# One pool of eight PSUM banks, and the scores of two query tiles in one stretch, in an attention kernel with a mixture of experts

## The chip, the cores and the metric

The kernel runs on one core of a Trainium2 chip. Its engines work side by side, each through its own queue in order: TensorE (PE; its weight loads are shown apart as PEld), VectorE (DVE), ScalarE (ACT), GpSimd (POOL) and SyncE (SP), which issues the DMAs. TensorE writes to PSUM alone, which has eight banks of 512 float32 columns by 128 partitions; VectorE and ScalarE read from there. The metric is the time of the device in microseconds. Everything here is float32.

## The reference: what is computed

Two blocks in a row, over 4 batches of 1088 rows. The first is a linear attention with a sketch of the features; its output, 128 columns wide, is the input `x` of the second: causal attention by four experts, of which each row uses the two with the largest gate.

```python
a = einsum('rd,bhsd->bhsr', S1, x); b = einsum('rd,bhsd->bhsr', S2, x)   # phi: 64 products a row
...
num = einsum('bhsf,bhfd->bhsd', q_p, kv); den = einsum('bhsf,bhf->bhs', q_p, z)[..., None] + 1e-06
x = num / den                                   # (B, S, H*D) = (4, 1088, 128)
for e in range(4):                              # experts, 64 wide
    q = x @ wq[e]; k = x @ wk[e]; v = x @ wv[e]
    scores = where(causal, -1e9, (q @ k.T) / 8)
    a = exp(scores - scores.max(-1)); a /= a.sum(-1) + 1e-09
    out += gate[e] * (a @ v @ wo[e])            # gate: softmax over the two best of x @ w_gate
```

## The kernel before: tiling, order and names

**Tiles.** The experts are taken in two pairs (`g` = 0, 1; the two of a pair are `e` = 0, 1, one in partitions 0 to 63, the other in 64 to 127). The 1088 queries of a batch are cut into tiles `i` of 128: eight whole ones and one of 64. Two whole tiles (2p, 2p+1) form a group `p`. For tile `i` the scores cover the keys 0 to 128 (i + 1), since later ones are masked.

**Steps of one tile.** `scores` (L400) makes the products of queries and keys in PSUM (`sc`, L412), in pieces of 512 keys. `soften` (L393) reads them once on VectorE (L395: adds the mask, writes the negated scores to `a` in SBUF and their minimum to `mx`) and once on ScalarE (L398: the exponential, with its sum in `z`). `turns_of` (L469) transposes `a` on TensorE, up to four blocks of 128 x 128 into one bank `tp` (L477), and `evacuate` copies the bank to `aT` in SBUF: two copies of three on ScalarE (L72), the third on VectorE (L70). `values` (L546) multiplies `aT` by the values into a bank `av` (L552), `gates` (L494) makes the factors (gate over sum, product on POOL at L501) and transposes them into the same bank (L507), ScalarE copies these to `rs` (L509), and VectorE multiplies `av` by `rs` into `yT` (L557), which frees the bank. `output` (L614) projects `yT` through `wo` into a bank `po` (L619), and the copy of it goes out by a DMA of SP.

**PSUM.** Two pools. `ps_sc` has two buffers of two banks each, for scores alone; a tile of more than 512 keys takes both, one for each expert. `ps_tp` has four buffers of one bank, for everything else: transposes, values, outputs, and all steps that prepare the next batch (`kps`, `qps`, `tq`, `num`, `tx`, `qk`, `vg` and others, in `prepare`, L206).

**Units.** TensorE's order is written out by hand; the other engines' order is made by the framework's scheduler. A batch is a list of units (`units`, L529):

- "Q": tiles 0 and 1, both expert pairs (`scores_first`, L421)
- "P": tiles 2 and 3 of one pair
- "G": a larger group (tiles 4 and 5, or 6 and 7) of one pair
- "L": the last tile of 64 rows, both pairs at once (`scores_last`, L441)

Batches 0 to 2 run Q, P, P, G, G, G, G, L. The last batch runs P, P, A, B, A, B, L, A, B, A, B, Q, where "A" and "B" are the two tiles of a large group as units of their own. For each unit the loop does: scores (for "G" of the first tile alone), values of units that are ready, for "G" the scores of its second tile, and then the `jobs`: transposes left over from the unit before, output projections, and for "G" the transposes of its first tile; between the jobs stand pieces of the preparation of the next batch (`spend`). Then "G" transposes its second tile. "A" and "B" transpose half of their tile at once and leave the other half to the next unit. "L", and "Q" of the last batch, run the jobs left over before their own scores. In the last batch the preparation's pieces are used up in the first two units.

Of the kernel before, what the change touches and what calls it, by code (L numbers as in the profile page):

```python
# [10 lines left out]
F32 = mybir.dt.float32  # L11
BF16 = mybir.dt.bfloat16
I32 = mybir.dt.int32
ALU = mybir.AluOpType
ACTF = mybir.ActivationFunctionType
# [4 lines left out]
def kernel(  # L20
# [20 lines left out]
    nc = tc.nc  # L41
    B, H, S, D = q.shape
# [7 lines left out]
    NG = E // 2  # L50
    scale = 1.0 / math.sqrt(HD)
# [3 lines left out]
    p4 = ctx.enter_context(tc.tile_pool(name="p4", bufs=4))  # L55
    ps_sc = ctx.enter_context(tc.tile_pool(name="ps_sc", bufs=2, space=bass.MemoryType.PSUM))
    ps_tp = ctx.enter_context(tc.tile_pool(name="ps_tp", bufs=4, space=bass.MemoryType.PSUM))

# [8 lines left out]
    def evacuate(out_, in_):  # L67
        turn[0] += 1
        if turn[0] % 3 == 0:
            nc.vector.tensor_copy(out_, in_)  # L70
        else:
            nc.scalar.copy(out_, in_)  # L72


# [110 lines left out]
    mask = const("mask", [128, 1024], BF16)  # L185
# [20 lines left out]
    def prepare(b):  # L206
# [6 lines left out]
        n = NJ - 1  # L213

        def bank(name):
            return ps_tp.tile([128, 512], F32, tag="tp", name=name)

# [174 lines left out]

    def soften(a, src, msk, mx, z, most=3e38):  # L393

        nc.vector.tensor_tensor_reduce(out=a, in0=src, in1=msk, scale=-1.0, scalar=most,  # L395
                                       op0=ALU.add, op1=ALU.min, accum_out=mx)
        if z is not None:
            nc.scalar.activation(out=a, in_=a, func=ACTF.Exp, bias=mx, scale=-1.0, accum_out=z)  # L398

    def scores(b, i, g, qk, z):  # L400

        n = 128 * i + 128
        if n <= 512:
            t = ps_sc.tile([128, 2, 512], F32, tag="sc", name=f"sc{b}_{i}_{g}")
            sc = [t[:, e, :] for e in range(2)]
        else:
            sc = [ps_sc.tile([128, 1024], F32, tag="sc", name=f"sc{b}_{i}_{g}_{e}") for e in range(2)]
        for c0 in range(0, n, 512):
            c1 = min(c0 + 512, n)
            for e in range(2):  # L410
                rows = slice(64 * e, 64 * e + 64)
                nc.tensor.matmul(sc[e][:, c0:c1], qk[rows, g, 128 * i : 128 * i + 128], qk[rows, NG + g, c0:c1],  # L412
                                 start=True, stop=True)
        mx = p4.tile([128, 2], F32, tag="mx", name=f"mx{b}_{i}_{g}")
        width, tag, bufs = (512, "as", 8) if n <= 512 else (S, "a", 4)
        ats = [p4.tile([128, width], F32, tag=tag, name=f"a{b}_{i}_{g}_{e}", bufs=bufs) for e in range(2)]
        for e in range(2):
            soften(ats[e][:, 0:n], sc[e][:, 0:n], mask[:, 1024 - n :], mx[:, e : e + 1], z[:, e : e + 1])
        return ats

    def scores_first(b, qk, zs):  # L421

        made = [[[], []] for _ in range(NG)]
        for g in range(NG):
            t = ps_sc.tile([128, 2, 512], F32, tag="sc", name=f"sc{b}_0_{g}")
            for i in range(2):
                for e in range(2):
                    rows = slice(64 * e, 64 * e + 64)
                    nc.tensor.matmul(t[:, e, 128 * i : 256 * i + 128], qk[rows, g, 128 * i : 128 * i + 128],  # L429
                                     qk[rows, NG + g, 0 : 128 * i + 128], start=True, stop=True)  # L430
            mx = p4.tile([128, 2, 2], F32, tag="mx0", name=f"mx{b}_0_{g}")
            a = [p4.tile([128, 512], F32, tag="as", name=f"a{b}_0_{g}_{e}", bufs=8) for e in range(2)]
            for i in range(2):
                for e in range(2):
                    n, dst = 128 * i + 128, a[e][:, 128 * i : 256 * i + 128]
                    soften(dst, t[:, e, 128 * i : 256 * i + 128], mask[:, 1024 - n :], mx[:, i, e : e + 1],
                           zs[g][:, i, e : e + 1])
                    made[g][i].append(dst)
        return made

    def scores_last(b, qk, z):  # L441

        sc = [ps_sc.tile([128, 1024], F32, tag="sc", name=f"sc{b}_8_{e}") for e in range(2)]
        ext = [ps_tp.tile([128, 512], F32, tag="tp", name=f"ext{b}_{e}")[:, 0:64] for e in range(2)]

        def some(dst, e, c0, c1):
            rows = slice(64 * e, 64 * e + 64)
            for g in range(NG):
                nc.tensor.matmul(dst[64 * g : 64 * g + 64], qk[rows, g, 1024:], qk[rows, NG + g, c0:c1],  # L449
                                 start=True, stop=True)  # L450

        for e in range(2):
            some(ext[e], e, 1024, S)
        for c in range(0, 1024, 512):
            for e in range(2):
                some(sc[e][:, c : c + 512], e, c, c + 512)
        mx = p4.tile([128, 4], F32, tag="mx8", name=f"mx{b}_8")
        ats = [p4.tile([128, S], F32, tag="a", name=f"a{b}_8_{e}") for e in range(2)]
        for e in range(2):
            soften(ats[e][:, 1024:], ext[e], mask_last, mx[:, 2 + e : 3 + e], None)  # L460
        for e in range(2):

            most = mx[:, e : e + 1]
            nc.vector.tensor_tensor_reduce(out=ats[e][:, 0:1024], in0=sc[e], in1=mask[:, 0:1].to_broadcast([128, 1024]), scale=-1.0,
                                           scalar=mx[:, 2 + e : 3 + e], op0=ALU.add, op1=ALU.min, accum_out=most)
            nc.scalar.activation(out=ats[e], in_=ats[e], func=ACTF.Exp, bias=most, scale=-1.0, accum_out=z[:, e : e + 1])
        return ats

    def turns_of(name, i, ats, aT, q0):  # L469

        def some(e0, e1, j0, j1):
            tp = ps_tp.tile([128, 512], F32, tag="tp", name=f"tp{name}_{e0}_{j0}")
            nk, nj = size(j0), j1 - j0
# [55 lines left out]
    def units(b, qk, vt, gw, gw8):  # L529
# [3 lines left out]


        for p in range((NJ - 1) // 2) if b < B - 1 else (1, 3, 2, 0):
# [3 lines left out]
            for g in range(NG):  # L539
# [6 lines left out]
                def values(p=p, g=g, aT=aT, yT=yT, name=name):  # L546
                    av = ps_tp.tile([128, 512], F32, tag="tp", name=f"av{name}")
                    for j in range(2 * p + 2):
# [22 lines left out]
                if p == 0:  # L571
                    four.append((z, turns, close))
                elif p == 1:
                    yield "P", make, turns, [close]
                elif b < B - 1:
                    yield "G", make, turns, [close]
                else:
                    yield "A", make, turns, []
                    yield "B", make, turns, [close]
            if four:  # L580
# [6 lines left out]
    def last_unit(b, qk, vt, gw8):  # L587
# [5 lines left out]
        def values():  # L593
            av = ps_tp.tile([128, 512], F32, tag="tp", name=f"av{b}_8")
            for g in range(NG):
# [18 lines left out]
    def output(b, p, yT):  # L614
        nq, n = (128, 2) if p < NJ // 2 else (64, 1)
        po = ps_tp.tile([128, 512], F32, tag="tp", name=f"po{b}_{p}")
        for x in range(n):
# [9 lines left out]
    with tc.manual_schedule(engines={mybir.EngineType.PE}):  # L627

        warm = ps_tp.tile([128, 512], F32, tag="tp", name="warm")
        for _ in range(16):  # L630
# [13 lines left out]
        for b in range(B):  # L644
# [16 lines left out]
            for n, (kind, make, turned, close) in enumerate(units(b, *now)):  # L661
                jobs, turns = turns + done, []
                if kind == "L" or kind == "Q" and b == B - 1:
                    for f in jobs:
                        f()
                    jobs = []
                    groups += turning
                    turning = []
                made = {x: make(x) for x in ((0, 1) if kind == "P" else (1,) if kind == "B" else (0,))}
                ends = do_values()  # L670
                spend(0.0, columns=True)
                if kind == "G":
                    made[1] = make(1)
                    jobs += turned(made, 0)
                done = [f for finish, to_gate in ends for f in finish(to_gate)]
                if b + 1 < B:
# [10 lines left out]
                if kind == "G":  # L687
                    turns = turned(made, 1)
                    cut = len(turns)
                else:  # L690
                    turns = [f for x in made for f in turned(made, x)]
                    cut = len(turns) // 2 if kind in "AB" and len(turns) > 2 else 0
                for f in turns[:cut]:
                    f()
                turns = turns[cut:]
                (groups if kind == "G" else turning).extend(f() for f in close)
# [39 lines left out]
```

## Time and profile before

| | |
|---|---|
| median of 3 runs | 398.3 us (398.27 to 398.81) |
| profiled execution, its time | 398.61 us |
| its span, first to last instruction | 396.8 us |
| busy from 0 to 40 us (start-up): TensorE, VectorE, ScalarE | 34.2, 30.0, 15.0 us |
| busy from 40 to 311.8 us (271.8 us) | 261.1, 160.2, 161.4 us |
| busy from 311.8 us to the end (last batch, 85.0 us) | 77.9, 44.5, 50.2 us |

How to read what follows: rows of the page's groups have the line, the engine, the operation, output and inputs by name, shapes, the count, then busy time and mean ns of one, then the idle time of the engine just before and what ended it. A float32 product shows as two rows on TensorE, and the rows of the two experts run side by side in two halves of the array. The length of a TensorE row holds its way through the array, so rows overlap and a busy TensorE need not be streaming at its best.

These are the largest groups of score work on the page's account and in the list of groups by shape:

| group | count | mean ns | busy us |
|---|---|---|---|
| transposes `tp`, 128 x 128 | 640 | 276 | 89.1 |
| values `av`, 256 columns | 512 | 384 | 62.0 |
| scores `sc`, 512 columns | 192 | 624 | 51.3 |
| copies `aT` on ScalarE, 512 columns | 85 | 586 | 47.8 |
| copies `aT` on VectorE, 512 columns | 43 | 690 | 29.7 |
| exponential, all shapes | 128 | 767 | 98.1 |

### The profile page before, as it was taken

How to read it: one execution, taken by the hardware profiler on the slowest of the kernel's cores; microseconds unless marked ns; L12 is line 12 of the kernel's file. 1: busy time of each engine (PE TensorE's matmuls, PEld its weight loads, DVE VectorE, ACT ScalarE, POOL GpSimd, SP SyncE). 2: the span in 40 equal slices, each digit the busy share in tenths (PEclk: the TensorE clock that was granted, in tenths of full speed). 3: DMA queues.
4: the chain of work that ended last, by engine and by line, in shares of the span. 5: the costliest groups of instructions: out<-in, count | busy, mean ns of one | idle time of the engine just before them, and what ended most of it. 6: DMA issues, size and time to landing. Idle time of an engine off the chain costs nothing.

```text
span 396.8 us, 8017 instructions
## 1 busy us (share of the span) xinstructions
PE 373.2 (94%) x3152; PEld 265.4 (67%) x3152; DVE 234.6 (59%) x661; ACT 226.5 (57%) x550; POOL 58.7 (15%) x87
## 2 busy tenths in 40 slices
PE   8898999999999999999999999999999999999995
PEld 7764687667665776767664767766756475666673
DVE  6867866555548675366456564555655844745551
ACT  2236666555666656456475656754665565656582
POOL 3400461000001740000000541000000010000010
PEclk9999999999999999999999999999999999999999
DMA  7705022000000000000000000000000000000000
GB/s 192 200 2 170 16 98 71 2 1 15 13 2 0 15 2 5 15 0 15 1 15 0 2 13 7 13 2 0 15 13 2 1 16 6 0 15 2 15 4 26
DMA packets 11349, 9.95 MB, mean 25 GB/s; under 512 B 3632, under 2 KB 10288, under 8 KB 11312
## 3 DMA queue, kind: packets, MB, share of 16 engines
q1 hardware_dynamic: 11296, 9.44, 8.6%
q8 instruction: 24, 0.39, 0.4%
q14 instruction: 13, 0.11, 0.1%
q10 hardware_dynamic: 16, 0.00, 0.0%
HBM read 7.22 MB, written 2.23 MB: 24 GB/s over the span
## 4 chain that ended last, share of the span: by engine, by line
PE 72%; DVE 15%; ACT 9%; issue 2%; DMA 2%; SPq 0%; ACTq 0%; DVEq 0%
PE av L552 16%; PE sc L412 15%; PE tp L477 14%; DVE a L395 7%; ACT a L398 7%; PE qk L326 5%; PE vg L338 3%; PE num L300 3%; PE po L619 3%; PE av L600 3%; PE sc L449 2%; DMA qin<-in_q_dram 2%; DVE qT L223 1%; PE sc L429 1%; PE qps L251 1%
## 5 line engine op out<-in xcount | busy, mean ns | idle before, releaser
L398 ACT ACTIVATE a<-a,mx 128x256 f32<-128x256 f32 (+7 forms) x128 | 98.1, 767 | 59.6 <-DVE mx L395 59.2
L395 DVE CUSTOM_DVE_ANT_0 a<-sc,mask 128x256 f32<-128x256 f32 (+7 forms) x128 | 90.2, 754 | 64.1 <-PE sc L412 62.1
L477 PE MATMUL tp<-ident,a 128*128 128x128 f32 (+1 forms) x648 | 90.1, 276 | 10.6 <-DVE yT L557 6.8
L477 PEld LDWEIGHTS tp<-ident,a 128*128 128x128 f32 (+1 forms) x648 | 72.8, 142 | 26.0 <-DVE yT L557 10.2
L72 ACT COPY aT<-tp 128x512 f32<-128x512 f32 (+3 forms) x119 | 61.6, 544 | 17.9 <-PE tp L477 17.2
L552 PE MATMUL av<-aT,vt 128*64 128x256 f32 (+1 forms) x640 | 67.9, 362 | 0.0
L412 PE MATMUL sc<-qkT 64*128 64x512 f32 (+3 forms) x320 | 67.7, 541 | 0.0
L501 POOL TENSOR_TENSOR rb<-gw,r 128x256 f32<-128x256 f32 (+1 forms) x36 | 21.1, 589 | 297.2 <-DVE r L498 227.2
L552 PEld LDWEIGHTS av<-aT,vt 128*64 128x64 f32 x640 | 43.2, 137 | 31.0 <-issue 10.0
L70 DVE COPY aT<-tp 128x512 f32<-128x512 f32 (+3 forms) x61 | 38.6, 633 | 21.4 <-PE tp L477 21.3
L412 PEld LDWEIGHTS sc<-qkT 64*128 64x128 f32 x320 | 27.9, 186 | 23.7 <-issue 19.9
L326 PE MATMUL qk<-xT,wqk 128*128 128x512 f32 x64 | 31.1, 602 | 0.0
L509 ACT COPY rs<-av 128x256 f32<-128x256 f32 (+1 forms) x36 | 12.1, 356 | 27.7 <-PE av L507 27.6
L398 ACT ACTIVATION_READ_ACCUMULATOR a<-a,mx 128x1 f32 x128 | 23.9, 187 | 0.0
L619 PE MATMUL po<-wo,yT 128*128 128x128 f32 (+1 forms) x144 | 20.4, 281 | 1.7 <-DVE yT L557 1.5
L338 PE MATMUL vg<-wvg,xT 128*128 128x260 f32 (+1 forms) x72 | 20.2, 392 | 1.5 <-DVE vt L70 1.5
L497 DVE TENSOR_SCALAR r<-z 128x4 f32<-128x4 f32 (+1 forms) x36 | 6.3, 176 | 23.5 <-ACT a L398 16.6
L72 ACT COPY qkT<-qk 128x512 f32<-128x512 f32 x20 | 11.7, 585 | 14.4 <-PE qk L326 14.1
L619 PEld LDWEIGHTS po<-wo,yT 128*128 128x128 f32 (+1 forms) x144 | 17.3, 185 | 3.5 <-DVE yT L557 1.9
L300 PE MATMUL num<-kvz,qpT 128*128 128x66 f32 x144 | 17.9, 273 | 0.2 <-ACT qpT L72 0.2
L300 PEld LDWEIGHTS num<-kvz,qpT 128*128 128x128 f32 x144 | 17.1, 192 | 0.9 <-ACT qpT L72 0.5
L326 PEld LDWEIGHTS qk<-xT,wqk 128*128 128x128 f32 x64 | 10.7, 190 | 8.4 <-issue 4.7
(118 smaller groups left out, 392.0 us busy)
## 6 DMA issues: line engine op xcount, KB each, us to landing
kin<-in_k_dram SPq DMA_DIRECT2D x4, 544.0 KB, 4.0
qin<-in_q_dram SPq DMA_DIRECT2D x4, 544.0 KB, 5.1
vin<-in_v_dram SPq DMA_DIRECT2D x16, 128.0 KB, 5.7
out_dram<-ob SPq DMA_DIRECT2D x16, 128.0 KB, 1.8
vtl<-in_v_dram SPq DMA_DIRECT2D x8, 16.0 KB, 3.4
wqk<-in_moe_wq_dram SPq DMA_DIRECT2D x1, 128.0 KB, 5.3
wqk<-in_moe_wk_dram SPq DMA_DIRECT2D x1, 128.0 KB, 3.2
wvg<-in_moe_wv_dram SPq DMA_DIRECT2D x1, 128.0 KB, 3.1
```

Of the source, the lines that this page charges most:

```text
L70: nc.vector.tensor_copy(out_, in_)
L72: nc.scalar.copy(out_, in_)
L300: nc.tensor.matmul(num[:, 66 * (y - 2 * x0) : 66 * (y - 2 * x0) + 66], qpT[:, y], kvz[:, y % 2].rearrange("p h d -> p (h d)"), start=True, ...
L326: nc.tensor.matmul(t, wt(a), xT[:, 512 * c : 512 * c + 512], start=True, stop=True)
L338: nc.tensor.matmul(t[0:m, 0 : E * HD + E], xT[:, 128 * j : 128 * j + m], wvg, start=True, stop=True)
L395: nc.vector.tensor_tensor_reduce(out=a, in0=src, in1=msk, scale=-1.0, scalar=most, op0=ALU.add, op1=ALU.min, accum_out=mx)
L398: nc.scalar.activation(out=a, in_=a, func=ACTF.Exp, bias=mx, scale=-1.0, accum_out=z)
L412: nc.tensor.matmul(sc[e][:, c0:c1], qk[rows, g, 128 * i : 128 * i + 128], qk[rows, NG + g, c0:c1], start=True, stop=True)
L477: nc.tensor.transpose(tp[0:nk, x : x + 128], ats[e][:, 128 * j : 128 * j + nk], ident)
L501: nc.gpsimd.tensor_tensor(out=rb[:, 0 : w // 128].rearrange("p x (e d) -> p x e d", d=HD), in0=gws[:, :, :, None].to_broadcast(wide), in1= ...
L552: nc.tensor.matmul(av[HD * e : HD * e + HD, lo:256], vt[:, j, c : c + HD], aT[:, e, j, lo:256], start=(j == 0), stop=(j == 2 * p + 1))
L619: nc.tensor.matmul(po[0:nq, DM * x : DM * x + DM], yT[:, g, 128 * x : 128 * x + nq], wo_sb[:, g], start=(g == 0), stop=(g == NG - 1))
```

## The change

The two pools become one, of eight buffers of one bank, and every step takes single banks from it. Scores of more than 512 keys are read from PSUM in pieces, one for each bank: `soften` is split into `take` (VectorE, one for each piece; a later piece starts its minimum from that of the piece before) and `soften` (ScalarE, once over the whole row). In the last tile the 64 keys of the end are its third piece, where they were the first.

"G" makes the scores of both its tiles in one stretch, ahead of the values; the transposes of the first tile stay among the jobs, those of the second tile behind them. The units "A" and "B" are gone: the last batch runs P, P, G, G, L, G, G, Q. "L" and the last "Q" no longer run older jobs before their scores.

```diff
-    ps_sc = ctx.enter_context(tc.tile_pool(name="ps_sc", bufs=2, space=bass.MemoryType.PSUM))
-    ps_tp = ctx.enter_context(tc.tile_pool(name="ps_tp", bufs=4, space=bass.MemoryType.PSUM))
+    ps = ctx.enter_context(tc.tile_pool(name="ps", bufs=8, space=bass.MemoryType.PSUM))
...
+    def bank(name):
+        return ps.tile([128, 512], F32, tag="bank", name=name)
...
-    def soften(a, src, msk, mx, z, most=3e38):
+    def take(dst, src, msk, mx, most=3e38):
 
-        nc.vector.tensor_tensor_reduce(out=a, in0=src, in1=msk, scale=-1.0, scalar=most,
+        nc.vector.tensor_tensor_reduce(out=dst, in0=src, in1=msk, scale=-1.0, scalar=most,
                                        op0=ALU.add, op1=ALU.min, accum_out=mx)
-        if z is not None:
-            nc.scalar.activation(out=a, in_=a, func=ACTF.Exp, bias=mx, scale=-1.0, accum_out=z)
+
+    def soften(a, mx, z):
+
+        nc.scalar.activation(out=a, in_=a, func=ACTF.Exp, bias=mx, scale=-1.0, accum_out=z)
...
+        for c in range(0, n, 512):
+            keys = slice(c, min(c + 512, n))
+            sc = [bank(f"sc{b}_{i}_{g}_{c}_{e}")[:, 0 : keys.stop - c] for e in range(2)]
             for e in range(2):
                 rows = slice(64 * e, 64 * e + 64)
-                nc.tensor.matmul(sc[e][:, c0:c1], qk[rows, g, 128 * i : 128 * i + 128], qk[rows, NG + g, c0:c1],
+                nc.tensor.matmul(sc[e], qk[rows, g, 128 * i : 128 * i + 128], qk[rows, NG + g, keys],
                                  start=True, stop=True)
...
+            for e in range(2):
+                m = mx[:, e, c // 512 : c // 512 + 1]
+                take(ats[e][:, keys], sc[e], mask[:, 1024 - n + c : 1024 - n + keys.stop], m,
+                     mx[:, e, 0:1] if c else 3e38)
+                if keys.stop == n:
+                    soften(ats[e][:, 0:n], m, z[:, e : e + 1])
         return ats
...
-                elif p == 1:
-                    yield "P", make, turns, [close]
-                elif b < B - 1:
-                    yield "G", make, turns, [close]
                 else:
-                    yield "A", make, turns, []
-                    yield "B", make, turns, [close]
+                    yield "P" if p == 1 else "G", make, turns, [close]
...
-                jobs, turns = turns + done, []
-                if kind == "L" or kind == "Q" and b == B - 1:
-                    for f in jobs:
-                        f()
-                    jobs = []
-                    groups += turning
-                    turning = []
-                made = {x: make(x) for x in ((0, 1) if kind == "P" else (1,) if kind == "B" else (0,))}
+                made = {x: make(x) for x in ((0, 1) if kind in "PG" else (0,))}
                 ends = do_values()
                 spend(0.0, columns=True)
+                jobs = turns + done
+                done = [f for finish, to_gate in ends for f in finish(to_gate)]
+                turns = [f for x in made for f in turned(made, x)]
                 if kind == "G":
-                    made[1] = make(1)
-                    jobs += turned(made, 0)
-                done = [f for finish, to_gate in ends for f in finish(to_gate)]
+                    jobs += turns[: len(turns) // 2]
...
                 if kind == "G":
-                    turns = turned(made, 1)
-                    cut = len(turns)
-                else:
-                    turns = [f for x in made for f in turned(made, x)]
-                    cut = len(turns) // 2 if kind in "AB" and len(turns) > 2 else 0
-                for f in turns[:cut]:
-                    f()
-                turns = turns[cut:]
+                    for f in turns[len(turns) // 2 :]:
+                        f()
+                    turns = []
                 (groups if kind == "G" else turning).extend(f() for f in close)
```

More of the change, by code (lines that the diff above doesn't have):

```diff
@@ L213, in prepare @@
         n = NJ - 1
-        def bank(name):
-            return ps_tp.tile([128, 512], F32, tag="tp", name=name)
         abS = {}
@@ L400, in scores @@
     def scores(b, i, g, qk, z):
         n = 128 * i + 128
-        if n <= 512:
-            t = ps_sc.tile([128, 2, 512], F32, tag="sc", name=f"sc{b}_{i}_{g}")
-            sc = [t[:, e, :] for e in range(2)]
-        else:
-            sc = [ps_sc.tile([128, 1024], F32, tag="sc", name=f"sc{b}_{i}_{g}_{e}") for e in range(2)]
-        for c0 in range(0, n, 512):
-            c1 = min(c0 + 512, n)
+        mx = p4.tile([128, 2, 2], F32, tag="mx", name=f"mx{b}_{i}_{g}")
+        width, tag, bufs = (512, "as", 8) if n <= 512 else (S, "a", 4)
@@ L410, in scores @@
+        ats = [p4.tile([128, width], F32, tag=tag, name=f"a{b}_{i}_{g}_{e}", bufs=bufs) for e in range(2)]
+        for c in range(0, n, 512):
+            keys = slice(c, min(c + 512, n))
+            sc = [bank(f"sc{b}_{i}_{g}_{c}_{e}")[:, 0 : keys.stop - c] for e in range(2)]
             for e in range(2):
                 rows = slice(64 * e, 64 * e + 64)
-                nc.tensor.matmul(sc[e][:, c0:c1], qk[rows, g, 128 * i : 128 * i + 128], qk[rows, NG + g, c0:c1],
+                nc.tensor.matmul(sc[e], qk[rows, g, 128 * i : 128 * i + 128], qk[rows, NG + g, keys],
@@ L413, in scores @@
                                  start=True, stop=True)
[L414 to L418, printed above, removed]
+            for e in range(2):
[4 more added lines that the diff above has]
+                    soften(ats[e][:, 0:n], m, z[:, e : e + 1])
@@ L424, in scores_first @@
         for g in range(NG):
-            t = ps_sc.tile([128, 2, 512], F32, tag="sc", name=f"sc{b}_0_{g}")
+            sc = [bank(f"sc{b}_0_{g}_{e}") for e in range(2)]
             for i in range(2):
@@ L428, in scores_first @@
                     rows = slice(64 * e, 64 * e + 64)
-                    nc.tensor.matmul(t[:, e, 128 * i : 256 * i + 128], qk[rows, g, 128 * i : 128 * i + 128],
+                    nc.tensor.matmul(sc[e][:, 128 * i : 256 * i + 128], qk[rows, g, 128 * i : 128 * i + 128],
                                      qk[rows, NG + g, 0 : 128 * i + 128], start=True, stop=True)
@@ L434, in scores_first @@
                 for e in range(2):
[L435 to L438, printed above, removed]
+                    n, cols = 128 * i + 128, slice(128 * i, 256 * i + 128)
+                    m = mx[:, i, e : e + 1]
+                    take(a[e][:, cols], sc[e][:, cols], mask[:, 1024 - n :], m)
@@ L439, in scores_first @@
+                    soften(a[e][:, cols], m, zs[g][:, i, e : e + 1])
+                    made[g][i].append(a[e][:, cols])
         return made
     def scores_last(b, qk, z):
[L443 to L450, printed above, removed]
@@ L452, in scores_last @@
-        for e in range(2):
-            some(ext[e], e, 1024, S)
-        for c in range(0, 1024, 512):
-            for e in range(2):
[L456 to L466, printed above, removed]
+        mx = p4.tile([128, 2, 3], F32, tag="mx8", name=f"mx{b}_8")
@@ new lines, in scores_last @@
+        ats = [p4.tile([128, S], F32, tag="a", name=f"a{b}_8_{e}") for e in range(2)]
+        for c in range(3):
+            keys = slice(512 * c, min(512 * c + 512, S))
+            sc = [bank(f"sc{b}_8_{c}_{e}")[:, 0 : keys.stop - 512 * c] for e in range(2)]
+            for e in range(2):
+                rows = slice(64 * e, 64 * e + 64)
+                for g in range(NG):
+                    nc.tensor.matmul(sc[e][64 * g : 64 * g + 64], qk[rows, g, 1024:], qk[rows, NG + g, keys],
+                                     start=True, stop=True)
+            for e in range(2):
+                m = mx[:, e, c : c + 1]
+                take(ats[e][:, keys], sc[e], mask[:, 0:512] if c < 2 else mask_last, m,
+                     mx[:, e, c - 1 : c] if c else 3e38)
+                if c == 2:
+                    soften(ats[e], m, z[:, e : e + 1])
@@ L471, in some @@
         def some(e0, e1, j0, j1):
-            tp = ps_tp.tile([128, 512], F32, tag="tp", name=f"tp{name}_{e0}_{j0}")
+            tp = bank(f"tp{name}_{e0}_{j0}")
             nk, nj = size(j0), j1 - j0
@@ L546, in values @@
                 def values(p=p, g=g, aT=aT, yT=yT, name=name):
-                    av = ps_tp.tile([128, 512], F32, tag="tp", name=f"av{name}")
+                    av = bank(f"av{name}")
                     for j in range(2 * p + 2):
@@ L593, in values @@
         def values():
-            av = ps_tp.tile([128, 512], F32, tag="tp", name=f"av{b}_8")
+            av = bank(f"av{b}_8")
             for g in range(NG):
@@ L615, in output @@
         nq, n = (128, 2) if p < NJ // 2 else (64, 1)
-        po = ps_tp.tile([128, 512], F32, tag="tp", name=f"po{b}_{p}")
+        po = bank(f"po{b}_{p}")
         for x in range(n):
@@ L627 @@
     with tc.manual_schedule(engines={mybir.EngineType.PE}):
-        warm = ps_tp.tile([128, 512], F32, tag="tp", name="warm")
+        warm = bank("warm")
         for _ in range(16):
@@ L687 @@
                 if kind == "G":
-                    turns = turned(made, 1)
-                    cut = len(turns)
-                else:
-                    turns = [f for x in made for f in turned(made, x)]
-                    cut = len(turns) // 2 if kind in "AB" and len(turns) > 2 else 0
-                for f in turns[:cut]:
-                    f()
-                turns = turns[cut:]
+                    for f in turns[len(turns) // 2 :]:
+                        f()
+                    turns = []
                 (groups if kind == "G" else turning).extend(f() for f in close)
```

## The prediction

> **What bounds it now.** The profile page comes first.
>
> ```profile
> PE 373.2 (94%) x3152; PEld 265.4 (67%) x3152; DVE 234.6 (59%) x661; ACT 226.5 (57%) x550; POOL 58.7 (15%) x87
> ...
> PEclk9999999999999999999999999999999999999999
> ...
> PE 72%; DVE 15%; ACT 9%; issue 2%; DMA 2%; SPq 0%; ACTq 0%; DVEq 0%
> ```
>
> The reader is to see three things. TensorE is the fullest engine. Its clock is full in every slice (1.00 in each stretch I asked for), so no clock effect has to be explained. And the chain that ended last is on TensorE for only 72%: VectorE and ScalarE hold it for 24%, so TensorE does not stream all the time. Cut into stretches, 40 us to 312 us has TensorE busy for 261.1 of 271.8 us, the last batch (312 to the end) for 77.9 of 85.0.
>
> The view of waits, for TensorE alone, says who held it up (us in total, times, longest):
>
> ```profile
> PE tp L477 <- DVE yT L557: 6.8, 11, 0.8
> PE kps L251 <- ACT aT L72: 1.6, 3, 0.8
> PE po L619 <- DVE yT L557: 1.5, 2, 0.8
> PE vg L338 <- DVE vt L70: 1.5, 2, 0.7
> ...
> PE tp L477 <- ACT aT L72: 0.9, 1, 0.9
> PE tp L477 <- ACT a L398: 0.8, 2, 0.5
> PE tp L477 <- DVE aT L70: 0.7, 2, 0.5
> PE tx L317 <- ACT aT L72: 0.6, 1, 0.6
> PE tp L477 <- DVE xs L307: 0.6, 1, 0.6
> ```
>
> A transpose `tp` reads no `yT`: it waits for it because the multiply into `yT` frees a bank of the pool of four. So do `kps`, `vg` and `tx` against copies of other tiles. Bank waits: 6.8 + 1.6 + 1.5 + 0.9 + 0.7 + 0.6 + 0.6, with 0.5 in smaller lines, make **13.2 us in 24 stalls**. The lost time is more. A row's end is modelled, and eight transposes in one run take 1.09 us with rows of 0.27, so the pitch is 0.11; a stall costs its gap plus 0.27 - 0.11 = 0.16 us. 13.2 + 24 x 0.16 = **17.0 us**. Waits for data are others: `po` on `yT` in the tail (1.5), and two transposes of the last batch on the exponential (`ACT a`, 0.8).
>
> The timeline of one large group (batch 2, second block of queries of 256, g = 1) shows how such a stall comes about (start, length, engine, line):
>
> ```profile
> 256.85 1.35 PE L412 MATMUL sc<-qkT 64*128 64x512 f32 x8
> ...
> 258.13 4.11 PE L552 MATMUL av<-aT,vt 128*64 128x256 f32 x40
> ...
> 262.17 1.56 PE L412 MATMUL sc<-qkT 64*128 64x512 f32 x8
> ...
> 263.76 0.96 DVE L395 CUSTOM_DVE_ANT_0 a<-sc,mask 128x768 f32<-128x768 f32 x1 [3.95 <-PE sc L412]
> ...
> 265.52 0.75 DVE L557 TENSOR_TENSOR yT<-av,rs 128x256 f32<-128x256 f32 x2
> ...
> 266.00 0.44 PE L477 MATMUL tp<-ident,a 128*128 128x128 f32 x2 [0.81 <-DVE yT L557]
> ```
>
> Scores of tile 0, values, scores of tile 1, transposes. VectorE sits idle for 3.95 us while the values run, then has both score passes of tile 1 (0.88 us pitch each) ahead of `yT`. Two `av` banks and two banks of transposes are the whole pool, so the next transpose waits for `yT`: 0.81 + 0.16 us.
>
> **The change, part by part** (for the profiled execution: span 396.8, with 398.61 around it, 1.8 more; the median of the runs is 398.3).
>
> *Scores in one stretch, batches 0 to 2.* Twelve groups "G" put tile 1's scores right behind tile 0's, before the values. VectorE then works through them while TensorE does values. For the group above: first pass about 1.15 us after the stretch begins (the second pair of rows starts at 257.38, 0.53 on, and streams 0.43; 0.16 for the end), all eight pieces 3.6 us later, so done at 4.8; values end at 2.6 + 4.0 = 6.6. `yT` finds VectorE free. For the longest group (896 and 1024 keys): pieces 4.7 us, done at 5.9, values of 2.5 to 3.4 us end at 5.9 to 6.8. Also one switch into a score stretch less: two rows of 512 columns of `qk` take 0.86 us (249.09 to 249.95), 0.43 each, so the score stretch 256.85 to 258.13 should stream 2 x 0.43 + 2 x 0.107 = 1.07 and took 1.28. The 0.21 is the price of a switch; 12 x 0.21 = 2.5 us.
> [...] The row: eight transposes with loads of 0.14 each at a pitch of 0.11, so these loads are hidden and the switch is what costs. [...]
>
> *One pool of eight.* The bank waits lose their reason where four banks were full. A "G" now needs up to eight banks for its scores at once: the last copies of transposes must be done by the time tile 1's scores start. In the group above the last copy ran from 257.00 to 257.59, 0.74 us after the stretch began, and tile 1 would start at 1.28 (1.7 for the longest). Its own margin is 0.5 to 1.0 us. `av` needs a fifth-oldest piece: the first pass frees a bank at about 1.8, `av` comes at 2.6 to 3.4. So I see no new wait there; bounds below. I take 80% of 17.0 as gone, 13.6: the two `vg` stalls of the start-up (1.8 with their 0.16) stand in a stretch where VectorE is busy 8.8 of 11 us and may only move, and a TensorE that arrives earlier meets some copies that are not done.
>
> *More passes on VectorE.* A tile of more than 512 keys takes two passes for one: 4 tiles x 2 g x 2 heads x 4 batches = 64 more, and the last tile three for two, 8 more. Price from rows (mean ns of one):
>
> ```profile
> L395 DVE CUSTOM_DVE_ANT_0 a<-sc,mask 128x640 f32<-128x640 f32 x16 | 12.6, 821 | 7.5 <-PE sc L412 7.5
> ...
> L395 DVE CUSTOM_DVE_ANT_0 a<-sc,mask 128x512 f32<-128x512 f32 x16 | 10.4, 688 | 0.0
> ...
> L395 DVE CUSTOM_DVE_ANT_0 a<-sc,mask 128x128 f32<-128x128 f32 x16 | 4.0, 286 | 2.0 <-PE sc L429 2.0
> ```
>
> Two passes in a row start 0.75 apart (258.23, 258.98) with 0.82 each, so 0.07 of a row overlaps: 0.62 + 0.22 for 0.75, plus 0.06 for the running minimum as an operand (the 1024-column pass with it has 1282 ns, without it 1222). That is 0.15 each, 72 x 0.15 = 10.8 us of VectorE. [...] Either way VectorE goes to 245 us of some 382, 64%, and I cost it at **nothing**: the values of 1.7 to 4 us behind the scores hide it. It costs where no values stand behind (first "G" of the last batch's second pass, one place): 4 x 0.15 = 0.6 us, and there 2 us of older transposes stand first. The exponential of head 0 begins later too (third pass instead of first): 2.8 us after the stretch begins for 2.3 in the shortest group; its transposes come after values.
>
> *The last batch.* Four pairs "A", "B" become four "G": eight score stretches become four (0.84), two value stretches join others (a switch again, taken at the same 0.2 each, 0.4), and the switches out of and into transposes around the three "A" without values, about 0.1 each: 1.5 us in all. Its bank waits are in the 17.0. The two waits for the exponential (0.8 + 2 x 0.16 = 1.1) come from an "A" whose transposes follow its scores at 2 us; a "G" has values or the older transposes between; I take half, 0.5. But ScalarE gets fuller here: for a group of 896 and 1024 keys four exponentials (4.9), `rs` (0.4) and two of three copies (8 x 2/3 x 0.57 = 3.0) stand beside about 10 us of TensorE. "L" and "Q" no longer run the older transposes first; nothing is saved but banks. Queues of SP and POOL: one output copy and the gates' product on POOL keep their places (POOL is 15% busy).
>
> *New waits.* No row shows a score that waits for a copy. Below: 0, since the copies end 0.5 us early. Above: a score behind an exponential, priced under the rivals. Nearest row: the 0.74. I take 0.1 for each of 16 groups, 1.6.
>
> **Sum:** 13.6 + 2.5 + 1.5 + 0.5 - 1.6 = 16.5. 398.6 - 16.5 = 382.1; on the median's scale 381.8, so **382**.
>
> **The rivals.** *(1) The stalls only move.* TensorE comes sooner to transposes whose exponentials or copies are not done. For it: ScalarE and VectorE hold 24% of the chain. Against it: both are idle 40% of the time, in gaps such as the 3.95. If a quarter of 17.0 goes: 4.3 + 4.0 = 8.3, **390**.
> *(2) The shared pool couples scores to copies.* A copy that ScalarE must do for tile 1's last banks is queued behind tile 0's exponential, which itself waits for VectorE. In the group above that exponential ends 259.99, 3.1 us after the stretch begins, the copy 0.6 later; tile 1, due at 1.3, starts 2.4 us late, and the values, `rs` and `yT` queued behind it with it. For: one queue order serves both. Against: the copy is ready 2 us before the exponential. In all twelve groups: 29 - 18 gained = 11 slower, **409**. It decides from 18/12 = 1.5 us a group.
> *(3) VectorE becomes the bound.* At 64% only within a stretch; it would show as `av` waiting for `a`. 16 x 0.6 = 9.6 given back: 382 + 10 = **392**; I count it with (1).
>
> **Chances.** Main 0.62 (376 to 387), rivals (1) and (3) 0.20 (387 to 397), no change 0.03, rival (2) 0.15. To hold 8 in 10 the range is 375 to 397. Within 0.2% (0.8 us, about what a measurement of this kernel can tell) 0.03; faster 0.82; slower 0.15.
>
> **What would show it.** Right: `tp <- DVE yT` gone from TensorE's waits, TensorE's idle time down by about 12, sixteen fewer stretches of `sc`, VectorE's score rows 72 more and about 10 us longer. Wrong: waits of `sc` or `av` for `aT` copies or for `a`; `tp` waiting for the exponential in many groups. If TensorE's waits are gone and the time has not fallen, my 0.16 and 0.21 are wrong.

## The result and the profile after

The changed kernel takes **375.1 us** (median of 4 runs, 373.7 to 376.2) against 398.3: a ratio of 0.941, interval 0.937 to 0.946. That is 23.2 us less, where 16.3 were forecast. The direction and the mechanism were right; the size was not, and the time lies at the very bottom of the range of 375 to 397 (by the ratio 374.9, just outside it). A second set of runs of the same kernel gave 373.9. The time goes with the granted clock: of the eight runs of both sets the two at 0.991 took 376.1 and 376.2 us, the six at 0.998 or more (called "at the full clock" below) 373.5 to 375.2, in the median 373.9, which is 24.4 less than before.

The page of the changed kernel, the lines that answer to those shown of before (busy us, share, rows; then the chain that ended last):

```profile
PE 361.4 (97%) x3152; PEld 267.0 (72%) x3152; DVE 242.7 (65%) x805; ACT 226.0 (61%) x550; POOL 58.6 (16%) x87
...
PE 85%; DVE 7%; ACT 3%; issue 2%; DMA 2%; SPq 0%; ACTq 0%
```

The span fell from 396.8 to 372.1 us, by 24.7, for the same 3152 rows of TensorE. Of these, 12.9 are idle time (23.6 before, 10.7 now) and 11.8 are busy time (373.2 before, 361.4 now). VectorE and ScalarE hold 10% of the last chain, where they held 24%. The reader is to see that nearly half of the gain was never shown as idle.

Cut where the scores of tile 2 begin and where the last batch begins (us, from the view of windows; the variant "pool alone" is the first experiment):

| stretch | before | pool alone | changed |
|---|---|---|---|
| start to the first scores of tile 2 | 40.6 | 39.0 | 38.5 |
| from there to the last batch | 271.2 | 255.5 | 252.6 |
| last batch | 85.0 | 82.9 | 81.1 |

In the middle stretch TensorE is busy for 251.8 of the 252.6 us.

The view of TensorE's waits after the change, its first seven lines (us, times, longest):

```profile
PE warm L620 <- DVE idle L105: 1.1, 1, 1.1
PE tp L472 <- ACT a L399: 1.0, 1, 1.0
PE kv L276 <- DVE kp L260: 0.8, 1, 0.8
PE qps L250 <- DVE qT L222: 0.8, 1, 0.8
PE po L608 <- DVE yT L551: 0.8, 1, 0.8
PE av L546 <- DVE mx L394: 0.8, 1, 0.8
PE tp L472 <- ACT aT L71: 0.5, 1, 0.5
```

`tp <- DVE yT`, 6.8 us before, is gone, and so is every other bank wait of the start-up and the three first batches but one (`av <- DVE mx`, 0.8, in batch 0). The group that the prediction worked through looks like this now (start, length, engine, line):

```profile
240.14 2.64 PE L412 MATMUL sc<-qkT 64*128 64x512 f32 x16
...
241.30 0.69 DVE L394 CUSTOM_DVE_ANT_0 a<-sc,mask 128x512 f32<-128x512 f32 x1 [1.23 <-PE sc L412]
...
242.72 4.11 PE L546 MATMUL av<-aT,vt 128*64 128x256 f32 x40
...
244.70 0.48 DVE L394 CUSTOM_DVE_ANT_0 a<-sc,mask,mx 128x256 f32<-128x256 f32 x1
...
247.64 0.76 DVE L551 TENSOR_TENSOR yT<-av,rs 128x256 f32<-128x256 f32 x2 [0.32 <-ACT rs L504]
...
248.12 0.38 PE L472 MATMUL tp<-ident,a 128*128 128x128 f32 x2
...
248.34 1.45 PE L299 MATMUL num<-kvz,qpT 128*128 128x66 f32 x12
```

The first pass of VectorE begins 1.16 us after the stretch and the eighth ends at 5.0, as forecast (1.15 and 4.8). `yT` comes to an idle VectorE, and the transpose at 248.12 waits for nothing.

### The profile page after: what moved, and what is told of

Same layout as the page of the kernel before. It is cut to its first block, busy times and chain, and to the rows that moved or that the text cites. A ratio compares the mean times of both kernels' runs of the same rounds, so it can differ in the third digit from the quotient of the medians.

```text
span 372.1 us, 8229 instructions
## 1 busy us (share of the span) xinstructions
PE 361.4 (97%) x3152; PEld 267.0 (72%) x3152; DVE 242.7 (65%) x805; ACT 226.0 (61%) x550; POOL 58.6 (16%) x87
## 4 chain that ended last, share of the span: by engine, by line
PE 85%; DVE 7%; ACT 3%; issue 2%; DMA 2%; SPq 0%; ACTq 0%
PE tp L472 17%; PE av L546 17%; PE sc L412 14%; PE qk L325 8%; PE vg L337 4%; PE num L299 4%; PE po L608 4%; PE av L589 3%; PE av L502 3%; ACT a L399 3%; PE sc L453 2%; PE tq L289 2%; PE sc L430 2%; DVE a L394 2%; DMA qin<-in_q_dram 2%
## 5 line engine op out<-in xcount | busy, mean ns | idle before, releaser
L399 ACT ACTIVATE a<-a,mx 128x256 f32<-128x256 f32 (+8 forms) x136 | 107.5, 791 | 73.1 <-DVE mx L394 73.1
L472 PE MATMUL tp<-ident,a 128*128 128x128 f32 (+1 forms) x648 | 87.1, 274 | 1.6 <-ACT a L399 1.0
L394 DVE CUSTOM_DVE_ANT_0 a<-sc,mask 128x512 f32<-128x512 f32 (+3 forms) x136 | 74.2, 593 | 17.2 <-PE sc L412 12.9
L472 PEld LDWEIGHTS tp<-ident,a 128*128 128x128 f32 (+1 forms) x648 | 73.9, 142 | 11.2 <-issue 4.4
L412 PE MATMUL sc<-qkT 64*128 64x512 f32 (+3 forms) x320 | 63.3, 530 | 0.0
L394 DVE CUSTOM_DVE_ANT_0 a<-sc,mask,mx 128x512 f32<-128x512 f32 (+3 forms) x72 | 38.3, 570 | 0.0
L399 ACT ACTIVATION_READ_ACCUMULATOR a<-a,mx 128x1 f32 x136 | 25.4, 187 | 0.0
L394 DVE DVE_READ_ACCUMULATOR2_ANT mx<- 128x1 f32 x216 | 18.0, 83 | 0.0
```

The lines of the kernel that those rows point to most:

```text
L394: nc.vector.tensor_tensor_reduce(out=dst, in0=src, in1=msk, scale=-1.0, scalar=most, op0=ALU.add, op1=ALU.min, accum_out=mx)
L412: nc.tensor.matmul(sc[e], qk[rows, g, 128 * i : 128 * i + 128], qk[rows, NG + g, keys], start=True, stop=True)
L472: nc.tensor.transpose(tp[0:nk, x : x + 128], ats[e][:, 128 * j : 128 * j + nk], ident)
```

## The experiments

Two theories stood against each other. **Theory 1, full banks:** four banks for everything but scores were the limit, and each stall cost more than was booked. **Theory 2, order:** VectorE's passes for tile 1 stood ahead of `yT`, and only the joined stretch takes them away.

**The pool alone.** The pool and the piecewise reads of the change, with the units and TensorE's order as before (A and B too):

```diff
-                else:
-                    yield "P" if p == 1 else "G", make, turns, [close]
+                elif p == 1:
+                    yield "P", make, turns, [close]
+                elif b < B - 1:
+                    yield "G", make, turns, [close]
+                else:
+                    yield "A", make, turns, []
+                    yield "B", make, turns, [close]
...
-                made = {x: make(x) for x in ((0, 1) if kind in "PG" else (0,))}
+                made = {x: make(x) for x in ((0, 1) if kind == "P" else (1,) if kind == "B" else (0,))}
...
+                if kind == "G":
+                    made[1] = make(1)
+                    jobs += turned(made, 0)
```

> One pool of eight banks and reads of the scores in pieces, but the units and the order of TensorE as before (A and B, scores of tile 1 behind the values). Theory 1 (full banks): the stalls on banks were the loss, and each cost more than the 0.16 us above its gap that was booked, so the pool alone brings most: 379 to 384 us. Theory 2 (order): the multiply into yT sits behind tile 1's passes on VectorE, and only the joined stretch takes it out of there: 388 us or more, tp <- DVE yT still among TensorE's waits.

Measured: 378.8 us, ratio 0.951 (0.948 to 0.953), at the lower end of what theory 1 gave. Theory 1 holds. The same group in this variant, where VectorE still has tile 1's passes ahead of `yT`:

```profile
247.81 1.56 PE L412 MATMUL sc<-qkT 64*128 64x512 f32 x8
...
250.60 0.48 DVE L394 CUSTOM_DVE_ANT_0 a<-sc,mask,mx 128x256 f32<-128x256 f32 x1
...
250.67 0.38 PE L472 MATMUL tp<-ident,a 128*128 128x128 f32 x2
...
251.01 0.42 DVE L551 TENSOR_TENSOR yT<-av,rs 128x256 f32<-128x256 f32 x1
```

`yT` is still late, behind the last pass at 250.60, but the transpose at 250.67 runs ahead of it: it has a bank. Before, the same transpose came after `yT` (265.52, then 266.00). Here is also where the booked size failed. This variant has the same number of score stretches as before, and its span is 377.3: 19.5 less. TensorE's idle time fell by 13.1 (23.6 to 10.5), close to the 13.2 of the view of waits, and none of those bank waits is left in this variant's view; its busy time fell by 6.4 (373.2 to 366.8). Over 24 stalls that is 0.27 us each beside the gap, where 0.16 was booked.

That the busy time belongs to the stalls can be seen row by row, since both kernels send the same rows in the same order, but for those of the last tile's scores. At each stall the stalled row starts later by its gap plus 0.16 us, as booked (in this group, before: transposes 1.41 us behind the `tq` rows ahead of them, 264.59 to 266.00; here 0.44, 250.23 to 250.67; so 0.97 for 0.81 + 0.16), and the rows just behind it lose 0.03 to 0.21 us more, which was not booked: 0.19 to 0.38 a stall beside the gap, about 6.2 us in all.

One thing was not separated here: this variant also takes single banks and reads the scores in pieces, and how much of its gain that has in the old order was not run.

**The order alone.** The old pools, with the joined "G" in all batches:

```diff
-                made = {x: make(x) for x in ((0, 1) if kind == "P" else (1,) if kind == "B" else (0,))}
+                made = {x: make(x) for x in ((0, 1) if kind in "PG" else (0,))}
...
-                elif b < B - 1:
-                    yield "G", make, turns, [close]
                 else:
-                    yield "A", make, turns, []
-                    yield "B", make, turns, [close]
+                    yield "P" if p == 1 else "G", make, turns, [close]
```

> The two pools as before (two buffers of two banks for scores, four banks for the rest), but G joined, in the last batch too. Theory 1: tile 1's scores find both buffers full and wait for tile 0's passes on VectorE, 1 to 1.7 us in each of 16 groups, which eats the gain: 395 to 412 us, sc <- DVE a among TensorE's waits. Theory 2: the joined stretch is the gain, 385 us or less.

Measured: 417.2 us, ratio 1.048 (1.046 to 1.050), 18.7 us slower, beyond even the range of theory 1. The view of waits (first line) and the joined stretch:

```profile
PE sc L412 <- DVE mx L395: 17.3, 16, 1.4
```

```profile
266.72 1.35 PE L412 MATMUL sc<-qkT 64*128 64x512 f32 x8
...
268.99 2.30 PE L412 MATMUL sc<-qkT 64*128 64x512 f32 x8 [0.92 <-DVE mx L395]
...
269.73 0.72 PEld L412 LDWEIGHTS sc<-qkT 64*128 64x128 f32 x5 [0.45 <-DVE mx L395]
```

One wait in each of 16 groups. The second tile's scores also take 2.30 us in place of 1.56: the second buffer comes free one pass later than the first, and the weight load at 269.73, 0.74 us behind the stretch's begin, waits for that pass. Before, the first four loads of that stretch were done within 0.30 us (from 262.17), and the rows of the two experts ran side by side. Theory 2 falls: joined scores without banks lose.

**Two pools of four single banks.** The changed kernel, with scores and the rest in separate pools:

```diff
-    ps = ctx.enter_context(tc.tile_pool(name="ps", bufs=8, space=bass.MemoryType.PSUM))
+    ps = ctx.enter_context(tc.tile_pool(name="ps", bufs=4, space=bass.MemoryType.PSUM))
+    ps_sc = ctx.enter_context(tc.tile_pool(name="ps_sc", bufs=4, space=bass.MemoryType.PSUM))
...
-            sc = [bank(f"sc{b}_{i}_{g}_{c}_{e}")[:, 0 : keys.stop - c] for e in range(2)]
+            sc = [sbank(f"sc{b}_{i}_{g}_{c}_{e}")[:, 0 : keys.stop - c] for e in range(2)]
```

> The changed kernel, but its eight banks in two pools of four, one for scores and one for the rest (the last 64 keys of the last tile in the second). If sharing is needed: tile 1's pieces wait for tile 0's passes, 0.7 to 1 us in each of 16 groups, and four banks again fill behind av: 385 to 392 us. If single banks and the order are enough: 375 to 378 us.

Measured: 404.9 us, ratio 1.016 (1.015 to 1.018). The sharing is needed, and its lack cost more than expected: 12 us beyond the upper end. The two largest of its waits on a bank or a pass:

```profile
PE sc L416 <- DVE mx L398: 5.2, 8, 1.3
PE vg L341 <- DVE vt L70: 1.5, 2, 0.7
```

The waits shown sum to little; again the second tile's scores take longer (2.17 us at 261.50, behind a wait of 0.56 for `mx`, where before they took 1.56), and TensorE's busy time is 382.3 us, 20.9 more than in the changed kernel; the `sc` rows alone have 79.0 for 63.3.

This variant and the order alone share the joined order and the split into four banks and four. They differ in the single banks and the reads in pieces, which are thus worth 12.3 us there (417.2 to 404.9); the sharing brings 29.8 more (to 375.1).

**Fewer banks.** Only the number in the one pool is changed, `bufs=8` to 7 and to 6.

> The changed kernel with seven banks in its one pool. If the pool has slack: 375 us, as with eight. If the eight pieces of a joined stretch are what fills it: the last of them waits for the first pass on VectorE in the eight groups of 768 to 1024 keys or all 16, 0.3 to 0.6 us each, 378 to 384 us.

> The changed kernel with six banks. If the joined stretch fills the pool: its last two pieces wait for the first two passes, 0.7 to 1.3 us in each of 16 groups, and av behind them: 385 to 397 us. If the pool has slack: within 2 us of the changed kernel.

Measured: 375.2 us with seven (ratio 0.941, 0.940 to 0.942), 383.1 with six (0.962, 0.959 to 0.965). Seven are nearly enough, although a joined stretch asks for eight: in the changed kernel's group above the first pass has ended at 241.99 us, before the eighth piece begins at 242.19. The eighth bank has a small effect that the medians hide, as half the runs of the changed kernel's first set had the lower clock. At the full clock seven banks take 1.3 us more (375.2 for 373.9; spans 372.7 to 373.5 for 371.6 to 372.4), and waits on a bank come in: `tp` on `aT` 1.3 us for 0.5, `vg` on `vt` 0.4, `sc` on `mx` 0.3. Six cost 8 us, less than was expected (385 to 397), and six in one pool still beat four and four by 22 us.

**One more pass on VectorE.** Behind each of the 72 added passes another of up to 128 columns, which reads and writes the same values:

```diff
+        if not isinstance(most, float):
+            extra.append(p4.tile([128, 1], F32, tag="again", name=f"again{len(extra)}"))
+            n = min(128, dst.shape[-1])
+            nc.vector.tensor_tensor_reduce(out=dst[:, 0:n], in0=src[:, 0:n], in1=msk[:, 0:n], scale=-1.0,
+                                           scalar=3e38, op0=ALU.add, op1=ALU.min, accum_out=extra[-1])
```

> The changed kernel with one more pass of up to 128 columns on VectorE after each of the 72 added passes: it reads the same scores and writes the same values again, 0.22 to 0.28 us each, 16 to 20 us of VectorE, ahead of the exponential. If added passes are hidden behind the values, as the prediction costs them: within 1 us of the changed kernel. If VectorE's time reaches the end: 4 us or more, in the joined stretches and in the last batch.

Measured: 377.2 us, ratio 0.947 (0.945 to 0.949), 2.2 to 3.4 over the changed kernel's two medians, 3.3 when both are taken at the full clock. That lies between the two expectations. VectorE is busy 16.8 us longer (259.5 for 242.7), so about four fifths are hidden. TensorE's largest waits of this variant:

```profile
PE tp L478 <- ACT aT L72: 1.9, 2, 1.1
PE tp L478 <- ACT a L405: 1.6, 1, 1.6
```

In the changed kernel these two are 0.5 and 1.0: 2.0 us more, and all of it in the last batch: 1.2 in its group without values (below), 0.8 in another, 27 us earlier.

**The old order in the last batch.** The changed kernel, with A and B, and the older jobs ahead of "L" and "Q", in batch 3 only (the yields of the first experiment).

> The changed kernel with the last batch in its old order (A and B, older jobs ahead of L and Q). By the sum of the prediction the last batch's order is worth 1.5 us of switches and 0.5 of waits: 377 us. If the new stalls of its group without values (2 us at 341 to 346 us of the changed kernel's trace) eat that: 374 to 376 us, no difference.

Measured: 377.4 us, ratio 0.947 (0.942 to 0.952). The medians differ by 2.3 to 3.5, but two of the four runs had a granted clock of 0.987. The two at the full clock are 375.6 and 375.8 against 373.7 and 374.0: about 1.8 us, near the 2.0 of the sum.

**What is left in the last batch.** The changed kernel's timeline there:

```profile
341.32 0.41 PE L472 MATMUL tp<-ident,a 128*64 128x128 f32 x2 [0.49 <-ACT aT L71]
...
341.65 0.69 DVE L394 CUSTOM_DVE_ANT_0 a<-sc,mask 128x512 f32<-128x512 f32 x1 [0.97 <-PE tp L472]
...
344.71 1.79 PE L472 MATMUL tp<-ident,a 128*128 128x128 f32 x12 [1.00 <-ACT a L399]
```

This is the group without values. Tile 1's first pass waits for transposes, as the last tile's rows still hold two of the four buffers of `a`, and so its exponential and its transposes are late. The variant runs the last tile's transposes and the older jobs ahead of this group's scores, and so has the last tile's values behind them:

```diff
+                if b == B - 1 and kind == "G" and not groups:
+                    for f in turns + done:
+                        f()
+                    turns, done = [], []
+                    groups += turning
+                    turning = []
                 made = {x: make(x) for x in ((0, 1) if kind in "PG" else (0,))}
```

> The changed kernel, but in the last batch the group without values (tiles 4 and 5 of the first pair) runs the older jobs ahead of its scores, so that the last tile's values follow its scores and the last tile's rows of a are free for its second tile. If the stalls at 341 to 346 us are that group's want of cover (TensorE waits 0.7, 1.2 and 0.2 us there, and about 0.3 us of refill): 2 to 2.5 us less than the changed kernel, 371.5 to 373 us at the full clock. If the stall only moves to the jobs run early: 374 us.

Measured: 372.6 us (372.2 to 372.8), ratio 0.934 (0.933 to 0.936): 1.3 less than the changed kernel at the full clock, where 2 to 2.5 were expected. Both waits of TensorE (0.5 and 1.0) are gone, so the stalls were that group's want of cover; one for `yT` came in (0.8 in the changed kernel, 1.5 now), which takes part of the gain back:

```profile
PE po L608 <- DVE yT L551: 1.5, 2, 0.8
PE warm L620 <- DVE idle L105: 1.1, 1, 1.1
```

A second form left the output projection among the jobs (only `turns` run early):

> As last_tile_first, but the output projection stays among the jobs behind the values; only the transposes of the last tile go ahead of the scores. In last_tile_first TensorE waits 0.7 us more for yT at a po than in the changed kernel. If that is the early projection: 0.7 to 0.9 us less than last_tile_first, 371.5 to 372 us. If the wait only changes its place: 372.5 us.

Measured: 372.6 us, ratio 0.935 (0.933 to 0.938), with the same 1.5 us at `po`, so the early projection is not its cause. The changed kernel on the same chip:

> The changed kernel once more, beside the one above on the same chip: 373.7 to 376.2 us, the spread going with the granted clock (0.99 in the longer runs).

Measured: 373.9 us, ratio 0.938 (0.936 to 0.940). So both forms are below both kernels, by about 1.3 us against the changed one. The interval of the first form ends below that of this run. That of the second overlaps it, but two of its five runs had a granted clock of 0.989; at the full clock its three spans are 370.5 us each, and this run's four 371.6 to 372.4.

## Why the prediction was wrong in size

- **"I take 80% of 17.0 as gone, 13.6"**, less 1.6 for new waits: 12.0 for the pool. This is the step that failed: the pool alone brought 19.5 us of span. Of the 7.5 us between them, 3.4 are the discount. It was not needed: all 13.2 us of bank gaps went, the two `vg` stalls of the start-up included, which I had thought might only move (that stretch is 1.6 us shorter with the pool alone). Another 2.6 are the price beside the gap, 0.27 us a stall in place of 0.16. The rest is the 1.6 of new waits, of which the pool alone shows none. What the price left out stands in the timeline of before, behind the stalled transposes at 266.00:

```profile
266.33 1.55 PE L300 MATMUL num<-kvz,qpT 128*128 128x66 f32 x12
267.72 0.60 PE L477 MATMUL tp<-ident,a 128*128 128x128 f32 x4
```

From the stalled transpose to the next four are 1.72 us (266.00 to 267.72), in the changed kernel 1.51 (248.12 to 249.63). So rows behind a stall come late too, by 0.21 in this place, and none of it is an idle gap.
- **"0.1 for each of 16 groups, 1.6"** of new waits: in the changed kernel two showed (0.8 for `av` in batch 0; 0.5 for a transpose in the last batch), 1.3 in the idle gaps. The size was about right, the places were not: no scores waited for a copy. Rival (2) did not occur, and with seven banks the scores waited for only 0.3 us.
- **The joined stretches, 2.5 + 1.5 + 0.5**: right, the first a little low. From the pool alone to the changed kernel the middle stretch loses 2.9 us for twelve groups. TensorE's busy time there falls by 3.3 (255.1 to 251.8), 0.28 a group where 0.21 was booked, and the new wait for `av` takes part of it back. The last batch loses 1.8, where 2.0 were booked. The row that the prediction read, loads of 0.14 us at a pitch of 0.11, is the same in the changed kernel: sixteen transposes from 338.86 us on take 1.97, a pitch of 0.11 with rows of 0.27, and a load has 142 ns on the mean.
- **VectorE's passes at nothing**: nearly right. VectorE is busy 8.1 us longer (242.7 for 234.6), where the rows gave 10.8, and with them the 245 us that the prediction weighs. The running minimum costs what was read off, 0.06 us: 746 ns for 512 columns with it, 687 without. By the extra pass, about a fifth of such work reaches the end (3.3 of 16.8 us); for 8.1 us that would be 1.6 us, an estimate. Two waits that are left in the changed kernel (0.5 and 1.0) sit in the one group that the prediction named as uncovered, where I had put 2 us of older transposes as cover. Those transposes were themselves what tile 1 waited for, through the buffers of `a`, which I had not counted.
- **Rivals.** (1) the stalls only move: no. (3) VectorE as the bound: no, 65%. Slower by the joined stretch: it was real, but in a kernel that I had not asked about, the order without the pool, at 417.2.

## What to carry to other kernels

When a full engine waits under the name of an instruction whose output it does not read, as `tp` on `yT` here (6.8 us before, none with one pool), look whether that instruction frees a buffer: count banks before changing the order, and try the pool alone. Book a stall of TensorE at its gap plus about 0.25 us here (0.27 on the mean with the pool alone, 0.19 to 0.38 row by row), since the rows behind it are late as well, and take the busy time for a given number of rows as a measure beside the idle time. A small shared pool can beat two private ones that are larger together: in the joined order six shared banks were 22 us better than four and four.

## What the runs showed that was not expected

- The granted clock is not full at the start of every run: the profiles of the second form (mean 0.989) and of the old order in the last batch (0.987) have 0.91 on the mean of the first 40 us, those of the changed kernel and of the kernel before 1.00. Behind 40 us the old order has 1.00, the second form 1.00 up to 291 us and 0.99 from there, as the changed kernel has in its last batch. The cause stays open.
- A bank that comes free one pass later makes a stretch of scores longer. In the order alone the second expert's first load came 0.74 us behind the begin of the stretch, which took 2.30 us for 1.56; these 0.74 us show in TensorE's rows as busy time, not as a wait.
